# Weight conversion with its addition on VectorE, the verdict's reader moved, and natural copies by VectorE transposes

## The chip, the cores and the metric

The kernel runs on one core of a Trainium2 chip. The engines are named as in the profile: PE (TensorE, matmul and transpose; PEld is its weight load), DVE (VectorE), ACT (ScalarE), POOL (GpSimd) and SP (SyncE, whose queue issues the loads and stores). The metric is the device time of one execution in microseconds, median of several runs.

## What is computed

Three stages follow one another. All inputs are float32 but the two weight matrices of the middle stage, which are float64.

```python
# attention with a decaying state, B=4, H=8, S=768, D=48
for t in range(S):
    cur = einsum('bhd,bhe->bhde', u * k[t], v[t])
    y[t] = einsum('bhd,bhde->bhe', r[t], state + cur)
    state = w[t][..., None] * state + einsum('bhd,bhe->bhde', k[t], v[t])
x = y as 3072 tokens x 384

# feed-forward, 384 -> 2048 -> 384
h = x @ w_in
x = (h * (1.0 / (1.0 + exp(-1.702 * h)))) @ w_out

# mixture: 8 experts x 4 slots; phi is 384 x 32
logits = x @ phi
d = softmax of logits over the tokens
slots = d.T @ x                     # 32 x 384
out_slots[e] = relu(slots[e] @ w1[e]) @ w2[e]
c = softmax of logits over the slots
return c @ out_slots
```

## The kernel before

The tokens form 6 blocks of 512 (4 units of attention each, 24 units). A unit's attention is worked out on all engines and ends with `xth`/`xtl`, its tokens transposed and split into a high and a low part. A block's feed-forward walks over 16 slices f of the hidden width: h (L746, nine matmuls of xth and xtl with the slice's weights), the activation on ACT (L750, L754), its low part `glgh` on DVE (L758), and x (L766 to L768, nine matmuls), added up over f. What a block yields goes on to the mixture.

**Conversion** (`conv_nodes`, L468 to L506). A float64 weight arrives as two 32-bit words. For each of the 16 slices SP loads 768 KB of words into one of two `raw` buffers (L477); ACT takes the high word's magnitude into `cq` (L482) and scales the low word in place (L483); DVE clamps (L486), shifts and masks (L490) and puts the sign back (L494); one engine adds the low word's bits (L498); ACT writes the high part of the weight (L501) and DVE the low part (L504). A `raw` buffer is free when the addition has read it.

**Mixture, per block** (`moe2_nodes`, L786 to L916). Three copies (L802 on DVE, L804 on ACT) bring the block's x out of PSUM into `x2t`, with the model width on the partitions. From x2t PE makes the logits lg (L833). The natural copy `x2g`, with tokens on the partitions, is made by 12 PE transposes (L815) and four evictions (L819 on DVE or L821 on ACT). DVE takes the running maximum mb, mrun (L840, L844), ACT copies lg to lt (L836), PE transposes lt (ln, L848), DVE takes the row maximum rm and lc (L853, L854) and after the exponentials on ACT the normalised cnat (L870 to L873); en (L877) and es (L880) lead to pp (L885), which multiplies es with x2g and goes into prun (L892). After block 4 `scrA` (L1061, L1062) splits cnat, for the transposes cp (L1067).

**Verdict.** Limits of the number range are gathered while the kernel runs; inside0 (L1017 to L1020, DVE) folds them into `cm`, inside1 (L1023, POOL) takes the maximum over partitions, and inside2 (L1027, DVE) reads it into `outside`, which later decides whether a slower, careful path runs.

**Order.** Instructions stand in a fixed row on each engine. A planner writes these rows before the kernel is built: each step has a cost, a due time (`pr`) and sometimes a choice of engines with a cost for each (`C2E` for the addition), and steps marked `port` on DVE are not planned beside POOL. CONV0 and CONVD set the due times of the conversions, ATTD those of the attention units. Each engine works through its row in order: a row that waits holds up the rows behind it.

## Time and profile before

| what | us |
|---|---|
| median of 3 runs | 634.65 (633.98 to 636.14) |
| the profiled execution, own time | 633.73 |
| its span in the profile | 631.9 |
| PE busy | 570.4 |
| DVE busy | 431.6 |
| ACT busy | 274.9 |
| POOL busy | 90.3 |

The mean granted clock of TensorE is 0.99. The profiled execution is 1.8 us longer than its span; a change of the span is a change of the time. Busy shares are means over stages: attention of the first units until 66.84, block 0 among conversions until about 158, blocks 1 to 4 beside the attention of later units, block 5 and the last stage of the mixture. A row of the timeline or of a group gives, in brackets or at its end, how long its engine was idle just before it, and whose end released it. The end of a matmul is modelled, and matmuls overlap, so PE's pace is the distance of their starts.

### The profile page before, as it was taken

What the parts mean: (1) busy time and instruction counts of PE and PEld (TensorE: products, weight loads), DVE (VectorE), ACT (ScalarE), POOL (GpSimd) and SP (SyncE); (2) the same over time, 40 slices, a digit from 0 to 9 for tenths busy, and PEclk for the clock granted to TensorE, in tenths of its full rate; (3) what the DMA queues carried; (4) which work ended last, traced back from release to release, by engine and by line L of the source; (5) the groups of instructions that cost most, each with busy time, mean ns of one, the idle gap of its engine ahead of it and who ended that gap; (6) DMA issues with size and microseconds to landing.
All of it is one profiled execution on the core that took longest, in us unless ns stands there. A gap on an engine that the chain in (4) does not pass through costs nothing.

```text
span 631.9 us, 12380 instructions
## 1 busy us (share of the span) xinstructions
PE 570.4 (90%) x5092; PEld 462.7 (73%) x5092; DVE 431.6 (68%) x830; ACT 274.9 (44%) x524; POOL 90.3 (14%) x83
## 2 busy tenths in 40 slices
PE   3446899979999999999999999999999969999992
PEld 2445688767889999778877787877788757887362
DVE  9999797899999998787669766787672323112301
ACT  5544566573834443543316432444242333324232
POOL 3121232221111111111012202111120000000000
PEclk9999999999999999999999999999999989999997
DMA  8776434632343333032223232330210294467747
GB/s 294 233 240 209 140 104 158 215 150 76 115 114 114 107 108 113 7 107 74 91 76 101 55 110 77 101 113 28 74 39 1 95 357 147 153 229 249 306 152 219
DMA packets 29475, 86.08 MB, mean 136 GB/s; under 512 B 3040, under 2 KB 12384, under 8 KB 29408
## 3 DMA queue, kind: packets, MB, share of 16 engines
q1 hardware_dynamic: 29408, 85.19, 41.0%
q8 instruction: 42, 0.69, 0.5%
q14 instruction: 25, 0.20, 0.1%
HBM read 80.46 MB, written 4.72 MB: 135 GB/s over the span
## 4 chain that ended last, share of the span: by engine, by line
PE 74%; DVE 14%; issue 4%; DMA 3%; ACT 2%; POOL 1%; SPq 0%; ACTq 0%; DVEq 0%
PE h L746 28%; PE x L766 10%; PE x L767 9%; PE x L768 9%; PE y L652 5%; DMA raw<-in_wf_dram 2%; PE y L654 2%; PE aps L600 2%; PE so L1142 2%; PE eh L1100 2%; PE xps L668 1%; DVE glgh L758 1%; DVE at L574 1%; DVE at L552 1%; PE fo L1182 1%
## 5 line engine op out<-in xcount | busy, mean ns | idle before, releaser
L746 PE MATMUL h<-xth,w 128*128 128x512 f32 (+1 forms) x672 | 205.9, 371 | 3.2 <-ACT w L501 2.0
L750 ACT ACTIVATE ghgh<-h 128x512 fp32r<-128x512 f32 (+1 forms) x112 | 60.0, 537 | 231.7 <-PE h L746 171.0
L746 PEld LDWEIGHTS h<-xth,w 128*128 128x128 f32 x672 | 123.2, 191 | 25.8 <-ACT w L501 2.1
L766 PE MATMUL x<-ghgh,w 128*128 128x512 f32 (+1 forms) x336 | 125.7, 374 | 0.0
L746 PE MATMUL h<-xtl,w 128*128 128x512 f32 (+1 forms) x336 | 122.3, 364 | 0.5 <-DVE xtl L682 0.5
L767 PE MATMUL x<-glgh,w 128*128 128x512 f32 (+1 forms) x336 | 121.7, 362 | 0.6 <-DVE glgh L758 0.4
L768 PE MATMUL x<-ghgh,w 128*128 128x512 f32 (+1 forms) x336 | 121.4, 361 | 0.0
L758 DVE TENSOR_TENSOR glgh<-g,ghgh 128x512 fp32r<-128x512 f32 (+1 forms) x112 | 73.5, 657 | 55.4 <-ACT g L754 54.2
L766 PEld LDWEIGHTS x<-ghgh,w 128*128 128x128 f32 x336 | 63.9, 190 | 11.2 <-issue 0.6
L652 PEld LDWEIGHTS y<-vs,st 128*64 128x64 f32 (+2 forms) x768 | 55.0, 151 | 22.8 <-issue 13.2
L767 PEld LDWEIGHTS x<-glgh,w 128*128 128x128 f32 x336 | 63.9, 190 | 10.5 <-DVE glgh L758 1.9
L746 PEld LDWEIGHTS h<-xtl,w 128*128 128x128 f32 x336 | 64.2, 191 | 9.9 <-DVE xtl L682 1.4
L768 PEld LDWEIGHTS x<-ghgh,w 128*128 128x128 f32 x336 | 63.7, 190 | 9.6
L652 PE MATMUL y<-vs,st 128*64 128x48 f32 (+2 forms) x768 | 61.7, 238 | 9.0 <-DVE ind L551 4.7
L754 ACT ACTIVATE g<-h 128x512 f32<-128x512 f32 (+1 forms) x112 | 59.8, 534 | 4.8 <-DVE glgh L758 3.9
L654 PE MATMUL y<-vs,st 128*48 128x48 f32 (+2 forms) x704 | 50.1, 229 | 0.2 <-ACT st L622 0.2
L659 DVE TENSOR_TENSOR vs<-y,fl 48x384 f32<-48x384 f32 x44 | 24.4, 555 | 37.1 <-PE y L654 36.4
L498 POOL TENSOR_TENSOR cq<-cq,raw 128x768 int32<-128x768 int32 x16 | 32.1, 2008 | 112.2 <-DVE cq L494 52.2
L582 POOL TENSOR_TENSOR nat<-nat 128x384 f32<-128x384 f32 x16 | 16.2, 1012 | 217.4 <-DMA nat<-in_nat_dram 133.7
L654 PEld LDWEIGHTS y<-vs,st 128*48 128x48 f32 (+2 forms) x704 | 44.1, 133 | 0.8 <-ACT st L622 0.6
L600 PE MATMUL aps<-at 48*64 48x64 f32 x768 | 23.6, 239 | 20.5 <-DVE at L574 13.0
L612 DVE TENSOR_TENSOR st<-aps,mask 64x256 f32<-64x256 f32 (+1 forms) x80 | 37.8, 472 | 4.7 <-PE aps L600 3.7
(143 smaller groups left out, 695.8 us busy)
## 6 DMA issues: line engine op xcount, KB each, us to landing
w<-in_w_dram SPq DMA_DIRECT2D x32, 768.0 KB, 5.9
nat<-in_nat_dram SPq DMA_DIRECT2D x24, 576.0 KB, 3.8
raw<-in_wf_dram SPq DMA_DIRECT2D x16, 768.0 KB, 5.3
at<-in_ark_dram SPq DMA_DIRECT2D x24, 512.0 KB, 5.0
at<-in_aw_dram SPq DMA_DIRECT2D x24, 448.0 KB, 4.0
vs<-in_vr_dram SPq DMA_DIRECT2D x48, 96.0 KB, 2.9
out_dram<-ot SPq DMA_DIRECT2D x12, 384.0 KB, 4.0
ubt<-in_ub_dram SPq DMA_DIRECT2D x1, 192.0 KB, 7.5
```

Of the source, the lines that this page charges most:

```text
L498: onto[e].tensor_tensor(a, a, words(0), op=ALU.add)
L600: pe.matmul(ab[p if four else 0][vl:vh, col:col + CH], t_[a_][lo:hi, 1, 4 * g + h], t_[a_][lo:hi, 0, 4 * g + h], start=True, stop=True)
L612: ve.tensor_tensor(S[0][vl:vh, p, n * g:n * g + n, 0:CH], t_[kap[p if four else 0]][al:ah, 0:n * CH].rearrange("p (h t) -> p h t", h=n), m ...
L652: pe.matmul(yps[vl:vh, cols], S[0][0:k1, p, h, 0:CH], rhs, start=True, stop=True)
L654: pe.matmul(sps[ol:oh, cols], S[0][0:k1, p, h, CH:ROWS], rhs, start=True, stop=True)
L746: pe.matmul(h[:, :wd], a, b, start=(k == 0), stop=(k == len(seq) - 1))
L750: ac.activation(t_[kgh][0], t_[kh][:, :wd], AF.Gelu_apprx_sigmoid)
L754: ac.activation(t_[kg], t_[kh][:, :wd], AF.Gelu_apprx_sigmoid)
L758: ve.tensor_tensor(gl, t_[kg], gh.bitcast(F32), op=ALU.subtract)
L766: pe.matmul(o, whi, gh, start=(f == 0), stop=False)
L767: pe.matmul(o, whi, gl, start=False, stop=False)
L768: pe.matmul(o, wlo, gh, start=False, stop=(f == NF - 1))
```

## The change

- **Conversion.** The clamp (L486) is gone. The magnitude on ACT is scaled by 2^-112 and also summed over each partition into `wchk` (16 columns of the buffer `mx`), which inside0 tests with three more small operations. The shift has no mask; the sign's mask is one bit.
- **Addition.** `C2E` names DVE alone; in before's row all 16 stood on POOL. On DVE it is one instruction over 1536 halves of the 768 words.
- **Natural copies.** For the blocks in XND (1 to 4) the PE transposes and evictions are replaced by 16 DVE instructions (`xt32`), each of which transposes 4 x 3 blocks of 32x32 from x2t straight to x2g. Blocks 0 and 5 stay as they were.
- **Verdict.** inside1 is planned at 11.5 us and due early; its reader inside2 also waits for nsi, a step of the last stage, and is due last.
- **Planner.** CONV0, CONVD 0, 6 become 6, 4; ATTD 6 becomes 3.

```diff
@@ -30,12 +30,15 @@
 EPS = 1e-9
 W_TINY, W_HUGE = 2.0 ** -15, 122879.9921875
 F_MOST = 2.0 ** 40
+W_MOST = 2.0 ** -96
 RAWB, CQB, NEW = 2, 3, 8

 WIDE = (T, T // 2, T, T, T, T)

 KTU = (2, 3, 4, 5)
-C2E = {"DVE": 1.16, "POOL": 1.95}
+
+XND = (1, 2, 3, 4)
+C2E = {"DVE": 0.96}
 RUKE = ({"DVE": 1.12}, {"POOL": 2.1})
 QVE = ({"DVE": 0.56}, {"POOL": 1.05})
 PIECES = (192, 192)
@@ -44,8 +47,8 @@
 SOON = "w0 r0 c0 n0 u w1 r1 v0 n1 v1 w2 r2 n2 v2 c1 w3 r3 n3 v3"

 FIRST, SECOND, PERIOD, LAG, AHEAD = 42.0, 150.0, 82.0, 4.2, 74.0
-CONV0, CONVD, CONVL = 0.0, 6.0, 16.0
-ATT0, ATTD = 3.0, 6.0
+CONV0, CONVD, CONVL = 6.0, 4.0, 16.0
+ATT0, ATTD = 3.0, 3.0
 LAT = {"PE": 0.3, "ACT": 0.25, "DVE": 0.2, "POOL": 0.2, "DMA": 2.2, "X": 0.0}
 SAME = {"PE": 0.0, "ACT": 0.2, "DVE": 0.12, "POOL": 0.1, "DMA": 2.2, "X": 0.0}
 FROM = {"PE": 1.9, "ACT": 2.0, "DVE": 1.0, "POOL": 1.0, "DMA": 0.9}
@@ -388,6 +391,7 @@
     tick = cst.tile([P, 1], F32, name="tick")
     mfin = cst.tile([P, 1], F32, name="mfin")
     sm = {n: cst.tile([P, NSL], F32, name=n) for n in ("big", "mx", "rz")}
+    wchk = sm["mx"][:, 0:NF]
     chk = sm["rz"][0:ROWS, 0:NU * NB]
     ubt = ap1.tile([P, DM], F32, name="ubt")
     ind = ap1.tile([ROWS, NH, CH], F32, name="ind")
@@ -479,19 +483,17 @@
         def c0():
             wt[f] = wp.tile([P, 2, 2 * DM], F32R, tag="w", name=f"w{f}")
             t_[cq] = cp1.tile([P, 2 * DM], F32, tag="cq", name=cq, bufs=CQB)
-            ac.activation(t_[cq], words(1).bitcast(F32), AF.Abs)
+
+            ac.activation(t_[cq], words(1).bitcast(F32), AF.Abs, scale=2.0 ** -112, accum_out=wchk[:, f:f + 1])
             ac.activation(words(0), words(0).bitcast(U32), AF.Copy, scale=2.0 ** -29)
-
-        def c1a():
-            ve.tensor_scalar(t_[cq], t_[cq], W_TINY, W_HUGE, op0=ALU.max, op1=ALU.min)

         def c1b():
             a = t_[cq].bitcast(I32)
-            ve.tensor_scalar(a, a, 3, 0x3FFFFFF8, op0=ALU.logical_shift_left, op1=ALU.bitwise_and)
+            ve.tensor_scalar(a, a, 3, None, op0=ALU.logical_shift_left)

         def c1c():
             a = t_[cq].bitcast(I32)
-            ve.scalar_tensor_tensor(a, words(1), -0x40000000, a, op0=ALU.bitwise_and, op1=ALU.bitwise_or)
+            ve.scalar_tensor_tensor(a, words(1), -0x80000000, a, op0=ALU.bitwise_and, op1=ALU.bitwise_or)

         def c2(e):
             a = t_[cq].bitcast(I32)
@@ -504,8 +506,7 @@
             ve.tensor_tensor(wt[f][:, 1], t_[cq], wt[f][:, 0].bitcast(F32), op=ALU.subtract)

         n = N("DMA", 2.2, load, pr=soon(f"c{f}", pr - CONVL), take=[("raw", raw)])
-        n = N("ACT", 2 * act(2 * DM), c0, [n], pr, take=[("cq", cq), ("w", wk)], use=[raw])
-        n = N("DVE", dve(2 * DM, 1920), c1a, [n], pr, use=[cq], port=True)
+        n = N("ACT", 2 * act(2 * DM) + 0.2, c0, [n], pr, take=[("cq", cq), ("w", wk)], use=[raw])
         n = N("DVE", dve(2 * DM, 1920), c1b, [n], pr, use=[cq], port=True)
         n = N("DVE", dve(2 * DM), c1c, [n], pr, use=[raw, cq], port=True)
         n = N(C2E, 0, c2, [n], pr, use=[raw, cq], port=True)
@@ -820,8 +821,18 @@
                 else:
                     ac.activation(x2g()[:, j, 0:DM], t_[kt][:, :DM], AF.Copy)

+            if u in XND:
+                continue
             xns.append(N("PE", 0.33, xn, ts, pr(3.5), take=psum(kt)))
             ev.append(N({"DVE": dve(DM), "ACT": act(DM)}, 0, xg, [xns[-1], grp_last.get("pp")], pr(7.2), use=[kt]))
+
+        def xt32(q, s):
+            src = x2t()[32 * q:32 * q + 32, :, :, 32 * s:32 * s + 32]
+            dst = x2g()[32 * s:32 * s + 32, :, 0:DM].rearrange("p j (c d) -> p j c d", c=KC)[:, :, :, 32 * q:32 * q + 32]
+            ve.transpose(dst, src)
+
+        if u in XND:
+            ev = xns = [N("DVE", 0.57, lambda q=q, s=s: xt32(q, s), ts + [grp_last.get("pp")], pr(50)) for q in range(4) for s in range(4)]
         grp_last["xn"] = xns
         mo, mn = mrun[(u + 1) % 2], mrun[u % 2]
         klg, kln, ken, kpp = (f"{k}{u}" for k in ("lg", "ln", "en", "pp"))
@@ -1014,10 +1025,13 @@


     def inside0():
-        t_["cm"] = m2["ep"].tile([P, 2], F32, name="cm")
+        t_["cm"] = m2["ep"].tile([P, 3], F32, name="cm")
         ve.memset(t_["cm"], -1.0)
         ve.tensor_scalar(chk, chk, F_MOST, -1.0, op0=ALU.is_le, op1=ALU.mult)
         ve.tensor_reduce(t_["cm"][0:ROWS, 0:1], chk, axis=AX.X, op=ALU.max)
+        ve.tensor_scalar(wchk, wchk, W_MOST, -1.0, op0=ALU.is_lt, op1=ALU.mult)
+        ve.tensor_reduce(t_["cm"][:, 2:3], wchk, axis=AX.X, op=ALU.max)
+        ve.tensor_tensor(t_["cm"][:, 0:1], t_["cm"][:, 0:1], t_["cm"][:, 2:3], op=ALU.max)

     def inside1():
         gp.partition_all_reduce(t_["cm"][:, 1:2], t_["cm"][:, 0:1], P, reduce_op=bass_isa.ReduceOp.max)
@@ -1029,9 +1043,8 @@
     def inside3():
         t_["rv"] = nc.values_load(t_["out"][0:1, 0:1], min_val=0, max_val=1, skip_runtime_bounds_check_because="one less a comparison's 0 or 1")

-    n = nin = N("DVE", 0.35, inside0, limits + [nep], tend - 70)
-    n = N("POOL", 0.57, inside1, [n], tend - 29)
-    nok = N("DVE", 0.1, inside2, [n], tend - 28)
+    n = nin = N("DVE", 0.75, inside0, limits + [nep], tend - 70)
+    nout = N("POOL", 11.5, inside1, [n], tend - 70)

     G = grp_last
     n = N("DVE", 0.07, f0, [G["mx"]], tend - 59)
@@ -1046,6 +1059,7 @@
     nsi = N("POOL", 0.68, si0, [nep], tend - 40, take=[("xl", "scrB")])
     nsi = nsi0 = N("DVE", 0.17, f7, [n6, nz, nsi], tend - 59, use=["sp", "scrB"])

+    nok = N("DVE", 0.1, inside2, [nout, nsi], tend + 40)
     finish[0](nsi)


```

The names in the rows below carry the number of their buffer; at, ind, aps, st, vs and nat are buffers of the attention. The lines of the changed kernel lie a few off: the shift is L492, the sign's or L496, the addition L500, the last subtraction L506, glgh L759, the DVE transposes L832. DVE in block 0, about two conversions, before:

```order
L490 TENSOR_SCALAR cq_782<-cq_782 128x768
L574 TENSOR_TENSOR at_520<-at_520 112x1024
L494 SCALAR_TENSOR_TENSOR cq_782<-raw_746,cq_782 128x768
L486 TENSOR_SCALAR cq_835<-cq_835 128x768
L612 TENSOR_TENSOR st_96<-aps_0_853,mask 64x8x64 x2
L758 TENSOR_TENSOR glgh_7_0_850<-g_7_0_872,ghgh_7_0_849 128x512
L490 TENSOR_SCALAR cq_835<-cq_835 128x768
L582 TENSOR_TENSOR nat_584<-nat_584 128x384
L583 TENSOR_TENSOR nat_584<-nat_584,ubt 128x384
L504 TENSOR_TENSOR w_781<-cq_782,w_781 128x768
L494 SCALAR_TENSOR_TENSOR cq_835<-raw_801,cq_835 128x768
```

The same place now:

```order
L492 TENSOR_SCALAR cq_738<-cq_738 128x768
L506 TENSOR_TENSOR w_699<-cq_700,w_699 128x768
L496 SCALAR_TENSOR_TENSOR cq_738<-raw_703,cq_738 128x768
L759 TENSOR_TENSOR glgh_4_0_723<-g_4_0_772,ghgh_4_0_722 128x512
L500 ISA cq_738<-raw_703,cq_738 128x1536
L613 TENSOR_TENSOR st_96<-aps_0_741,mask 64x8x64 x2
L492 TENSOR_SCALAR cq_800<-cq_800 128x768
L506 TENSOR_TENSOR w_737<-cq_738,w_737 128x768
L496 SCALAR_TENSOR_TENSOR cq_800<-raw_759,cq_800 128x768
L759 TENSOR_TENSOR glgh_5_0_780<-g_5_0_821,ghgh_5_0_779 128x512
L500 ISA cq_800<-raw_759,cq_800 128x1536
L759 TENSOR_TENSOR glgh_6_0_825<-g_6_0_861,ghgh_6_0_824 128x512
```

The clamps are gone, and behind each or (L496) the addition (L500) stands in DVE's own row, one glgh later.

DVE at the turn from block 4 to block 5, from the verdict's first row on, before:

```order
L1062 TENSOR_TENSOR scrA<-cnat,scrA 128x8x32
L1018 MEMSET cm 128x2
L1019 TENSOR_SCALAR rz<-rz 112x24
L1020 TENSOR_REDUCE cm<-rz 112x1
L1027 TENSOR_SCALAR outside<-cm 128x1
L840 TENSOR_REDUCE mb_5328<-lg_5304 128x1
L844 TENSOR_SCALAR mrun_83<-mb_5328,mrun_84 128x1
L819 COPY x2g<-x2t_0_5322 128x384
L758 TENSOR_TENSOR glgh_0_0_5320<-g_0_0_5326,ghgh_0_0_5319 128x512
L819 COPY x2g<-x2t_2_5351 128x384
```

The same place now, from the row maximum on (ahead stand the six rows of the verdict, four of the block's 16 transposes, mb and mrun, and four more transposes):

```order
L864 TENSOR_REDUCE rm_5343<-ln_5320 128x4
L865 TENSOR_TENSOR lc<-ln_5320,rm_5343 128x128
L832 STREAM_TRANSPOSE x2g<-x2t 32x4x3x32 x7
L881 TENSOR_REDUCE zr_5365<-lc 128x4
L882 TENSOR_SCALAR zr_5365<-zr_5365 128x4
L883 RECIPROCAL zr_5365<-zr_5365 128x4
L884 TENSOR_TENSOR cnat<-lc,zr_5365 128x128
L891 COPY es<-en_5361 128x128
L832 STREAM_TRANSPOSE x2g<-x2t 32x4x3x32
L1075 CAST scrA<-cnat 128x8x32
L1076 TENSOR_TENSOR scrA<-cnat,scrA 128x8x32
L759 TENSOR_TENSOR glgh_0_0_5296<-g_0_0_5309,ghgh_0_0_5295 128x512
```

The reader `outside` is gone from the head of the row, and glgh_0, which stood third behind mrun, now comes behind all 16 transposes and the chain to es.

PE at the same turn, behind the last matmul of h_1, before:

```order
L746 MATMUL h_1_0_5335<-xth_4751,w_248 128x512
L815 MATMUL x2t_2_5351<-ident,x2t 128x128 x3
L815 MATMUL x2t_3_5358<-ident,x2t 128x128 x3
L848 MATMUL ln_5365<-ident,lt 128x128
L766 MATMUL x_5_0_5367<-ghgh_0_0_5319,w_139 128x512
L767 MATMUL x_5_0_5367<-glgh_0_0_5320,w_139 128x512
L768 MATMUL x_5_0_5367<-ghgh_0_0_5319,w_139 128x512
```

and now:

```order
L747 MATMUL h_1_0_5299<-xth_4730,w_229 128x512
L859 MATMUL ln_5320<-ident,lt 128x128
L1081 MATMUL cp_5322<-ident,scrA 128x128 x4
L747 MATMUL h_2_0_5331<-xth_4730,w_270 128x512
...
L747 MATMUL h_2_0_5331<-xth_4730,w_270 128x512
L888 MATMUL en_5361<-ident,et 128x128
L896 MATMUL pp_5374<-x2g,es 32x385 x4
L1081 MATMUL cp_5382<-ident,scrA 128x128 x4
L767 MATMUL x_5_0_5390<-ghgh_0_0_5295,w_139 128x512
L768 MATMUL x_5_0_5390<-glgh_0_0_5296,w_139 128x512
```

The transposes are gone, h_2 and the matmuls en, pp and cp stand ahead of x(0) (L767), which stood right behind ln. In the turns from block 1, 2 and 3 glgh_0 and glgh_1 stand among the first eight transposes, and glgh_2 behind all 16.

## Rows read from the trace of the kernel before

Times are in us from the start of the span, means in ns.

**Rows 1.** The page: busy us of each engine, share of the span, instructions

```profile
PE 570.4 (90%) x5092; PEld 462.7 (73%) x5092; DVE 431.6 (68%) x830; ACT 274.9 (44%) x524; POOL 90.3 (14%) x83
```

**Rows 2.** Windows: us; busy PE, PEld, DVE, ACT, POOL; clock; DMA share; GB/s

```profile
0.00:66.84 66.84, 31.11 (x413) 26.32 (x413) 61.73 (x106) 31.27 (x56) 13.77 (x16) 1.00 0.75 243
66.84:158.50 91.66, 86.19 (x630) 69.61 (x632) 79.18 (x114) 56.13 (x95) 22.48 (x12) 1.00 0.42 137
158.50:250.50 92.00, 91.45 (x1130) 86.20 (x1127) 85.06 (x180) 43.86 (x105) 16.07 (x16) 1.00 0.36 110
500.00:520.00 20.00, 15.14 (x89) 11.73 (x88) 6.61 (x21) 9.34 (x17) 1.78 (x5) 0.91 0.87 333
```

**Rows 3.** Timeline, PE, L746: start, duration, operands, idle before, releaser

```profile
66.84 0.79 PE L746 MATMUL h<-xth,w 128*128 128x512 f32 x1 [0.58 <-ACT xth L679]
...
128.77 0.50 PE L746 MATMUL h<-xth,w 128*128 128x512 f32 x1 [1.96 <-ACT w L501]
```

**Rows 4.** Groups by form: count | busy us, mean ns | idle, releasers

```profile
L498 POOL TENSOR_TENSOR cq<-cq,raw 128x768 int32<-128x768 int32 x16 | 32.1, 2008 | 112.2 <-DVE cq L494 52.2 <-ACT st L622 21.9 <-DMA vs<-in_vr_dram 10.1
...
L494 DVE SCALAR_TENSOR_TENSOR cq<-raw,cq 128x768 int32<-128x768 int32 x16 | 15.2, 950 | 0.0
...
L486 DVE TENSOR_SCALAR cq<-cq 128x768 f32<-128x768 f32 x16 | 13.4, 835 | 4.4 <-ACT cq L482 4.2
...
L490 DVE TENSOR_SCALAR cq<-cq 128x768 int32<-128x768 int32 x16 | 8.8, 553 | 0.0
...
L570 ACT ACTIVATION_READ_ACCUMULATOR at<-at 112x1 f32 x24 | 4.8, 198 | 0.0
```

**Rows 5.** Timeline, 14.7 to 29 us: DVE rows beside additions on POOL

```profile
15.04 1.93 DVE L590 TENSOR_TENSOR nat<-nat,q 128x384 f32<-128x384 f32 x1
...
26.73 1.85 POOL L498 TENSOR_TENSOR cq<-cq,raw 128x768 int32<-128x768 int32 x1 [10.18 <-DVE cq L494]
...
27.19 1.81 DVE L486 TENSOR_SCALAR cq<-cq 128x768 f32<-128x768 f32 x1 [0.59 <-ACT cq L482]
```

**Rows 6.** Timeline, 107 to 110 us: an addition and the next raw load

```profile
107.47 2.11 POOL L498 TENSOR_TENSOR cq<-cq,raw 128x768 int32<-128x768 int32 x1 [5.69 <-DVE cq L494]
...
109.60 0.37 SPq L477 DMA_DIRECT2D raw<-in_wf_dram  x1
```

**Rows 7.** Waits, SyncE queue: us in total, times, longest

```profile
SPq L477 <- POOL cq L498: 47.8, 10, 9.8
```

**Rows 8.** Groups by line and form, three shapes on DVE

```profile
L574 DVE TENSOR_TENSOR at<-at 112x1024 f32<-112x1024 f32 x24 | 29.9, 1245 | 0.4
...
L637 DVE STREAM_TRANSPOSE st<-at 32x256 f32<-32x256 f32 x64 | 27.9, 435 | 1.4
...
L641 DVE STREAM_TRANSPOSE st<-at 32x32 f32<-32x32 f32 x32 | 5.1, 161 | 0.0
```

**Rows 9.** Timeline, PE, the turn from block 2 to block 3

```profile
340.96 0.82 PE L815 MATMUL x2t<-ident,x2t 128*128 128x128 f32 x6
...
341.61 0.27 PE L848 MATMUL ln<-ident,lt 128*128 128x128 f32 x1
```

**Rows 10.** Timeline, the turn from block 4 to block 5

```profile
500.87 1.97 ACT L804 ACTIVATE x2t<-x 128x512 f32<-128x512 f32 x3 [0.21 <-PE x L768]
...
512.57 0.15 DVE L1027 TENSOR_SCALAR outside<-cm 128x1 int32<-128x1 f32 x1 [9.94 <-POOL cm L1023]
...
513.28 0.42 PE L848 MATMUL ln<-ident,lt 128*128 128x128 f32 x1 [4.71 <-ACT lt L836]
...
513.37 0.77 PE L766 MATMUL x<-ghgh,w 128*128 128x512 f32 x1
...
520.11 0.39 PE L746 MATMUL h<-xtl,w 128*128 128x512 f32 x1
...
520.34 0.62 PE L746 MATMUL h<-xth,w 128*128 128x512 f32 x2
...
524.21 0.85 PE L885 MATMUL pp<-x2g,es 128*32 128x385 f32 x8
```

## The prediction, made before the changed kernel ran

> **What bounds the kernel now.** I read the page first, then windows, then groups by line and form, then waits and the timeline at two places. TensorE (PE) is busy 570.4 us of a span of 631.9 [rows 1], so only a stretch where PE waits, or work taken off PE, can shorten the run. The windows say where PE waits [rows 2]: up to 66.84 us it is busy 31.1 us while VectorE (DVE) is busy 61.73, so DVE carries that stretch; from 66.84, the first feed-forward matmul [rows 3], to 158.5, the end of block 0, PE is busy 86.19 of 91.66, so 5.5 us are idle; from 158.5 to 250.5 it is full (91.45 of 92.00) and DVE has 7 us to spare; in 500 to 520, the turn from block 4 to block 5, PE does 15.14 of 20. The change works in exactly these places, and the sum has four terms.
>
> **The conversion's prices.** Sixteen conversions run, each now clamp, shift, or, add, last subtraction [rows 4]. The clamp L486 goes: its free price is that of the shift L490, same shape, 0.553 us; its mean of 0.835 holds a stretch that the next paragraph explains. The shift without its mask and the other sign mask leave L490 and L494 as they are. ScalarE's L482 gets a read of its accumulator; the same read costs 0.198 at L570 [rows 4], so 16 x 0.2 = 3.2 us on an engine that works 31.27 of the first 66.84 us [rows 2], hidden but for 0.2 in each conversion's chain. The addition leaves GpSimd (POOL), 2.008 us x16, and becomes one row on DVE over 1536 halves of 768 words. No row of before shows it. Lower bound: 0.95, L494, the same 768 words with the same interleaved operand. Upper bound: one half per element at the rate of L574, 1.245 us for 1024 [rows 8], is 1.87. I take 0.95, because L494 is nearest in operands and words, and keep 1.87 for a rival. The Trainium skill, page "VectorE: DVE Perf Modes", section "What auto-detection actually checks", lets a two-source operation on 16-bit values run at twice the rate only where every tensor steps by one; the low words here are every second word, so by that rule the add runs at the single rate, and by the page's 0.96 GHz it would take an estimated 1.6 us and some overhead. That is rival two; no run here shows it yet.
>
> **Term 1, up to the first h matmul.** By the order, up to the last xtl of block 0 DVE issues 6 clamps, 6 shifts, 6 ors and 5 subtractions before, and 0, 5, 5 and 4 with 4 adds after; attention rows are equal in number. At 0.553 for clamp and shift and 0.95 for or and subtraction (which has the or's shape) that is 3.32 + 0.55 + 0.95 + 0.95 = 5.77 less, and 4 x 0.95 = 3.80 more: 1.97 less, or 1.7 when each of the 101 rows there before and of the 96 after is priced by its own group; I take 1.7. Besides, a POOL add slows the DVE row that it meets: L486 takes 1.81 at 27.19 beside the add of 26.73 [rows 5], 1.26 over its free price. Three such rows lie before 66.84; the first is L590 at 15.04, 1.93 where the others of its shape take 0.55, and they hold some 3.5 us (1.38, 1.26 and 0.9). With no add on POOL they fall away. 1.7 + 3.5 = 5.2, and since DVE carries this stretch it shows in full: the first h at about 61.6. Bounds: 1.5 with adds at 1.87 (4 x 0.92 dearer), 6 at most.
>
> **Term 2, block 0.** Two raw buffers feed the conversions; the next load is issued as the add ends (107.47 + 2.11, load at 109.60 [rows 6]), and SyncE's queue waits 47.8 us on the add in ten places [rows 7]. PE meets this as a late weight: 1.96 us idle before L746 at 128.77 [rows 3]. From load to load a conversion loses the clamp (0.84 with stretch) and 1.06 of the add, and gains 0.2: 1.7 shorter, with two buffers 0.85 per conversion, 8.5 for ten. PE can take back no more than its 5.5 us idle, and part of that is attention. The order also moves PE's attention work for units 6 and 7 from among block 0's matmuls to behind them: block 0 shortens and block 1, where PE is full, grows by as much, which enters the sum at nothing. I take 3.3, between 0 (the load, not the add, is late) and 6.
>
> **Term 3, three turns (blocks 1 to 3).** Before, PE transposes in 12 rows per block; six of them at 340.96 are followed by the next matmul at 341.61 [rows 9], 0.65, so 1.3 per block leaves a full PE. Four evictions go too, and 16 DVE transposes of 384 elements come. L637 has 256 in 0.435 and L641 32 in 0.161 [rows 8]: 1.22 ns an element, hence 0.59; 9.4 us per block, against 7 us of DVE's 92 that were idle from 158.5 to 250.5 and two or so that the evictions free: it fits, though narrowly. Bounds: 0.44 (256 elements alone), and above, 12 single blocks at 0.161, 1.93, which L637's 8 blocks in 0.435 speak against. They must be done before pp, the matmul that reads x2g. By the order, DVE has between the copies into x2t and es, which pp reads too, some 12 us: 9.4 of transposes, two glgh, and the small rows mb to cnat. PE has in front of pp lg, three h and two x (nine matmuls each, 0.23 us apart, 520.11 to 520.34 [rows 10], so five times 2.07) and some attention: about 12 us as well. It is just covered. 3 x 1.3 = 3.9; without cover each 0.1 us more per transpose puts 1.6 us before each pp.
>
> The same page, sections "The three transpose paths" and "Rules for kernel authors", tells authors to put a 128x128 transpose on TensorE when PSUM is a fitting destination, and gives VectorE 32x32 blocks only; this speaks against the change. Its 0.39 us on TensorE would make the 12 an estimated 4.7 us; the trace shows 12 in 1.3, and the row decides. What the rule threatens is rival three.
>
> **Term 4, the turn from block 4 to 5.** Before, the verdict's reader L1027 stood at 512.57 waiting 9.94 us for POOL, the maximum mb behind it, and PE waited 4.71 for lt until 513.28 [rows 10]. Moved back, it releases mb. But what is late next is the transposes. x2t is ready at 502.84 (500.87 + 1.97 [rows 10]). In DVE's new row stand, from 503.2 on (after six verdict rows): 4 transposes, mb and mrun, 4, rm and lc, 7, zr to cnat, es, 1, and only after two scrA rows glgh_0. At 15 x 0.59 + 0.5 + 0.6 + 0.9 + 0.3, es is done at 514.4; the last transpose frees pp at about 515.0, two scrA and glgh_0 x(0) at about 516.3. PE, with lg, h_1, ln, cp, h_2 and en in front, runs dry at about 510 (before at 513.28 - 4.71 = 508.57; less 1.3, plus h_2, cp and en): an idle of 5 us or more where 4.71 stood. But h_2, en, pp and two cp are done by then, which before came later: before, x(0), x(1), h_2, h_3 and pp were through at 525.06 (524.21 + 0.85); after, x(0), x(1) and h_3 end at 516.3 + 3 x 2.07 = 522.5, plus some 1.2 for the slow matmuls that follow such an idle (0.77 at 513.37 [rows 10]), 523.7. The gain is 1.4, that of the PE transposes (bounds -2 to 6). Moving the reader thus pays almost nothing itself. At its new place, after the last block's lc, its 0.15 us [rows 10] has POOL's result long before, and only a zr waits behind it.
>
> **Sum.** 5.2 + 3.3 + 3.9 + 1.4 = 13.8. From the profiled 633.73 that is 619.9; the median of the runs is 634.65, 0.92 higher, so 620.8.
>
> **Rivals.** One: term 4 keeps the whole wait. If the transposes run at 0.30, the 15 rows shrink by 4.4 us and the idle all but vanishes: 13.8 + 4.4 = 18.2, so 616.4. For: L641 shows 32 elements in 0.161, mostly fixed cost; against: L637's slope and the order. Two: the add costs 1.87. Term 1 falls to 1.5, and in block 0 eleven adds bring 10 us to a DVE busy 79.18 of 91.66 [rows 2], so term 2 is nought: 1.5 + 3.9 + 1.4 = 6.8, hence 627.9; for it, 1536 halves in the row; against, L494. Three, the slower side: DVE transposes with a destination scattered in 32-word pieces are dearer than 0.59 and stand before four pp. Sixty-four times the excess must eat 13.8, so from 0.59 + 0.22 = 0.81 on the kernel is slower; at 0.87 it is 17.9 - 13.8 = 4.1 slower, 638.8. For: no row has this shape; against: L637, eight blocks in one row, costs 0.054 a block. Four: the change doesn't act, because the run takes its fallback or PE's start hangs on loads (16 x 768 KB and attention's in 66 us at 243 GB/s, [rows 2]) rather than DVE, and the transposes' gain is lost at pp: 634 to 635.
>
> **How the numbers follow.** Forecast 0.55 (617 to 624.5, from terms 1 and 2 between their bounds), rival one 0.10 (612 to 617), two 0.22 (624.5 to 633), three 0.08, four 0.05. A measurement of this kernel tells some 0.3%, 1.9 us, from no change. Faster: 0.55 + 0.10 + 0.21 = 0.86; same: 0.05 + 0.01 = 0.06; slower 0.08. Leaving out three, four and the upper third of two (0.07), the range is 612 to 630.
>
> **What would show it.** Right: first h near 61.6 and no DVE row of 1.5 us or more beside an add; L500 near 0.95; L832 near 0.59; PE without idle at pp in the turns 1 to 3; at 4 to 5 an idle of about 5 us before pp or x instead of before ln. Wrong: L500 above 1.4 (rival two), L832 above 0.75 with idle before pp in four places (three), a first h later than 65, or an idle of under 1 us at 4 to 5 (one).

## The result, and the profile after

The changed kernel takes 616.37 us (median of 4 runs, 614.20 to 620.15); the kernel before, beside it, 635.39. The ratio is 0.9703 with a 95% interval of 0.9645 to 0.976, so 2.4 to 3.6% faster. Forecast were 620.8 us, 612 to 630. The profiled execution took 614.20 with a span of 612.4; it is the fastest of the four, so the profile shows the new kernel at its best.

The page's lines on the engines, the slices of PE, DVE and POOL, and the chain that ended last (of after, against [rows 1]):

```profile
PE 561.3 (92%) x5044; PEld 455.4 (74%) x5044; DVE 458.9 (75%) x889; ACT 274.5 (45%) x532; POOL 60.1 (10%) x67
...
PE   2565999999999999999999999999999969998992
...
DVE  9999997999998899998979998698963661212301
...
POOL 2000000000130121022120311111210000000000
...
PE h L747 29%; PE x L767 10%; PE x L768 10%; PE x L769 10%; PE y L653 5%; DVE x2g L832 3%; DMA raw<-in_wf_dram 3%; PE aps L601 2%; PE y L655 2%; PE so L1156 2%; PE eh L1114 2%; PE xps L669 1%; PE fo L1196 1%; DVE cq L500 1%; DVE glgh L759 1%
```

DVE works 27 us more and the kernel is 19.5 us shorter: what counted was where DVE stood in the way, not how much it did. POOL does 4.1 us of work up to 142.30, where 36 stood up to 158.50 before [rows 2], and the DVE transposes (L832) have come into the chain.

The stages up to block 2, as windows (of after, against [rows 2]; PE, PEld, DVE, ACT, POOL):

```profile
0.00:60.34 60.34, 29.46 (x412) 25.13 (x413) 56.30 (x99) 29.31 (x57) 4.01 (x11) 0.92 0.79 250
60.34:142.30 81.96, 80.81 (x566) 64.70 (x567) 74.31 (x113) 58.72 (x106) 0.11 (x1) 0.97 0.51 160
142.30:236.50 94.20, 94.20 (x1188) 89.73 (x1187) 85.66 (x184) 44.49 (x107) 14.98 (x17) 1.00 0.35 109
```

The groups on which the terms were built (of after, against [rows 4] and [rows 8]):

```profile
L832 DVE STREAM_TRANSPOSE x2g<-x2t 32x384 f32<-32x384 f32 x64 | 36.5, 570 | 1.0
...
L496 DVE SCALAR_TENSOR_TENSOR cq<-raw,cq 128x768 int32<-128x768 int32 x16 | 15.2, 952 | 0.1
L500 DVE CUSTOM_DVE_ANT_0 cq<-raw,cq 128x1536 uint16<-128x1536 uint16 x16 | 15.2, 950 | 0.0
...
L492 DVE TENSOR_SCALAR cq<-cq 128x768 int32<-128x768 int32 x16 | 8.8, 551 | 2.8 <-ACT cq L487 2.7
...
L487 ACT ACTIVATION_READ_ACCUMULATOR cq<-raw 128x1 f32 x16 | 3.1, 196 | 0.0
```

The three new prices are 0.950 us for the addition (taken as 0.95), 0.570 for a transpose (0.59) and 0.196 for the read of the accumulator (0.198).

**Where the time went.** To compare kernels I cut each profile at four marks that all of them have: the start of ACT's first activation (ghgh) of block 0, of block 2 and of block 5, and that of its last in block 5; the end of the span closes the last stage. Between the first two marks PE has the same work in both kernels, whatever the order moves inside. Times are from the timelines; stages in us.

| kernel | ratio to before | to block 0 | to block 2 | to block 5 | block 5 | rest |
|---|---|---|---|---|---|---|
| before | | 71.25 | 179.05 | 253.98 | 71.90 | 55.7 |
| changed | 0.9703 | 65.03 | 171.49 | 249.51 | 70.92 | 55.5 |
| difference | | -6.2 | -7.6 | -4.5 | -1.0 | -0.2 |
| forecast (terms 1 to 4) | | -5.2 | -3.3 | -3.9 | -1.4 | 0 |
| r1_plan_cost | 0.9638 | 65.96 | 170.82 | 249.56 | 64.21 | 57.5 |
| r2_xnd123_plan | 0.9634 | 66.46 | 171.00 | 249.54 | 65.11 | 56.3 |
| r3_reader_only | 0.9891 | 71.30 | 178.18 | 253.83 | 65.11 | 57.3 |
| r4_no_dve_transposes | 0.9708 | 65.75 | 171.45 | 253.28 | 65.88 | 57.7 |
| r5_add_on_pool | 0.9819 | 66.25 | 176.09 | 251.74 | 70.93 | 56.5 |
| r6_clamp_back | 0.9852 | 66.72 | 179.63 | 250.30 | 71.02 | 56.2 |
| r7_old_dates | 0.9811 | 74.98 | 170.33 | 251.18 | 71.15 | 56.9 |
| r8_new_dates_only | 1.0129 | 69.46 | 187.06 | 253.92 | 72.29 | 59.5 |
| r9_no_xnd_plan | 0.9722 | 66.54 | 174.85 | 253.34 | 65.12 | 59.4 |
| r10_double_transposes | 1.0143 | 65.96 | 171.12 | 284.62 | 65.12 | 57.4 |
| r11_clamp_gone | 0.9870 | 71.52 | 173.28 | 250.72 | 71.38 | 58.4 |
| r12_changed_again | 0.9712 | 65.45 | 173.85 | 249.53 | 70.22 | 56.3 |

The last three stages are sharp: kernels with the same order there agree within some 0.2 us to block 5 and 0.7 in block 5. The stage to block 2 is less so: among the seven kernels with the changed conversion and dates (changed, r1, r2, r4, r9, r10, r12) it goes from 170.82 to 171.49 in five and is 173.85 in r12 and 174.85 in r9. Those two have 3.4 us at a granted clock of 0.50 there (117.0 to 120.5 and 119.2 to 122.6), right behind an idle of PE of 1.43 and 1.75 us for glgh, and the other five have none. r3, r6 and r8 have such a stretch in that stage too, so 2 to 4 us of a difference to them can be this. All later marks of a kernel move with it. "Dates" are the planner's numbers CONV0, CONVD and ATTD.

### The profile page after: what moved, and what is told of

Same layout as the page of the kernel before. It is cut to its first block, busy times and chain, and to the rows that moved or that the text cites. A ratio compares the mean times of both kernels' runs of the same rounds, so it can differ in the third digit from the quotient of the medians.

```text
span 612.4 us, 12355 instructions
## 1 busy us (share of the span) xinstructions
PE 561.3 (92%) x5044; PEld 455.4 (74%) x5044; DVE 458.9 (75%) x889; ACT 274.5 (45%) x532; POOL 60.1 (10%) x67
## 4 chain that ended last, share of the span: by engine, by line
PE 77%; DVE 14%; DMA 3%; issue 2%; ACT 2%; SPq 0%; ACTq 0%; DVEq 0%
PE h L747 29%; PE x L767 10%; PE x L768 10%; PE x L769 10%; PE y L653 5%; DVE x2g L832 3%; DMA raw<-in_wf_dram 3%; PE aps L601 2%; PE y L655 2%; PE so L1156 2%; PE eh L1114 2%; PE xps L669 1%; PE fo L1196 1%; DVE cq L500 1%; DVE glgh L759 1%
## 5 line engine op out<-in xcount | busy, mean ns | idle before, releaser
L767 PE MATMUL x<-ghgh,w 128*128 128x512 f32 (+1 forms) x336 | 125.5, 374 | 0.0
L759 DVE TENSOR_TENSOR glgh<-g,ghgh 128x512 fp32r<-128x512 f32 (+1 forms) x112 | 72.4, 646 | 60.9 <-ACT g L755 59.4
L767 PEld LDWEIGHTS x<-ghgh,w 128*128 128x128 f32 x336 | 63.8, 190 | 11.0 <-issue 1.0
L653 PEld LDWEIGHTS y<-vs,st 128*64 128x64 f32 (+2 forms) x768 | 53.6, 149 | 16.6 <-issue 8.7
L755 ACT ACTIVATE g<-h 128x512 f32<-128x512 f32 (+1 forms) x112 | 59.6, 533 | 14.1 <-DVE glgh L759 13.8
L653 PE MATMUL y<-vs,st 128*64 128x48 f32 (+2 forms) x768 | 59.9, 236 | 2.2 <-DVE st L613 1.1
L601 PEld LDWEIGHTS aps<-at 48*64 48x64 f32 x768 | 20.1, 148 | 25.0 <-DVE at L575 16.9
L832 DVE STREAM_TRANSPOSE x2g<-x2t 32x384 f32<-32x384 f32 x64 | 36.5, 570 | 1.0
```

Source lines behind the costliest of these rows:

```text
L601: pe.matmul(ab[p if four else 0][vl:vh, col:col + CH], t_[a_][lo:hi, 1, 4 * g + h], t_[a_][lo:hi, 0, 4 * g + h], start=True, stop=True)
L653: pe.matmul(yps[vl:vh, cols], S[0][0:k1, p, h, 0:CH], rhs, start=True, stop=True)
L755: ac.activation(t_[kg], t_[kh][:, :wd], AF.Gelu_apprx_sigmoid)
L759: ve.tensor_tensor(gl, t_[kg], gh.bitcast(F32), op=ALU.subtract)
L767: pe.matmul(o, whi, gh, start=(f == 0), stop=False)
L832: ve.transpose(dst, src)
```

## The turn from block 4 to block 5: the reader, the transposes and one planned cost

In the new profile the wait is where the forecast put it (timeline; start, duration, idle before):

```profile
487.69 2.32 DVE L832 STREAM_TRANSPOSE x2g<-x2t 32x384 f32<-32x384 f32 x4
488.90 0.27 PE L859 MATMUL ln<-ident,lt 128*128 128x128 f32 x1
...
490.68 4.07 DVE L832 STREAM_TRANSPOSE x2g<-x2t 32x384 f32<-32x384 f32 x7
...
492.06 0.33 PE L888 MATMUL en<-ident,et 128*128 128x128 f32 x1 [0.36 <-ACT et L868]
...
495.73 0.28 DVE L891 COPY es<-en 128x128 f32<-128x128 f32 x1
496.03 0.58 DVE L832 STREAM_TRANSPOSE x2g<-x2t 32x384 f32<-32x384 f32 x1
...
496.75 1.51 PE L896 MATMUL pp<-x2g,es 128*32 128x385 f32 x8 [4.36 <-DVE x2g L832]
...
498.96 0.78 PE L767 MATMUL x<-ghgh,w 128*128 128x512 f32 x1
499.54 0.63 PE L768 MATMUL x<-glgh,w 128*128 128x512 f32 x1
```

ln no longer waits for POOL's maximum; PE runs dry behind en and waits 4.36 us for the last transpose, where 4.71 stood [rows 10]. The matmuls behind it are slow again (0.58 apart at first, where 0.23 is the pace). That is the granted clock, which stood at 0.50, the lower of its two levels (1.2 GHz). The windows (PE, PEld, DVE, ACT, POOL, clock), one of the kernel before and two of after:

```profile
513.40:516.80 3.40, 3.25 (x8) 2.26 (x9) 3.01 (x8) 3.37 (x8) 0.00 (x0) 0.50 1.01 418
```

```profile
496.75:501.40 4.65, 4.65 (x18) 2.92 (x19) 3.05 (x7) 1.19 (x2) 0.00 (x0) 0.50 0.45 183
501.40:504.00 2.60, 2.60 (x13) 2.15 (x12) 0.43 (x1) 1.09 (x2) 0.00 (x0) 1.00 0.25 31
```

In the kernel before PE had done nothing for 4.7 us and had just begun again when the clock fell, at 513.4; in the changed kernel it fell at 494.6, while PE waited. Half of what PE works at 0.50 is lost, an estimate from these windows: 1.6 us before and 2.3 after. Four runs take this place apart.

**The reader alone.** The kernel before, its reader moved:

```diff
-    nok = N("DVE", 0.1, inside2, [n], tend - 28)
+    nout = n
...
+    nok = N("DVE", 0.1, inside2, [nout, nsi], tend + 40)
     finish[0](nsi)
```

> The kernel before with nothing changed but the verdict's reader, which moves from the head of DVE's row to behind nsi. Theory: DVE no longer stands behind POOL's maximum, PE's 4.71 us idle before ln goes with the slow matmuls behind it: 5 to 6 us faster than before, near 629. Rival: lt, the exponentials or the evictions are late next and the wait only changes its name: under 2 us.

Measured: 627.02 us, 0.9891 (0.9873 to 0.9909), 6.7 us faster, and all of it in block 5: 71.90 to 65.11. The rows that had waited, now (timeline of r3_reader_only):

```profile
504.13 0.29 DVE L840 TENSOR_REDUCE mb<-lg 128x1 f32<-128x128 f32 x1 [2.48 <-PE lg L833]
...
507.43 0.27 PE L848 MATMUL ln<-ident,lt 128*128 128x128 f32 x1
...
510.98 0.38 POOL L1023 PARTITION_ALL_REDUCE cm<-cm  x1 [10.24 <-DVE scrA L1063]
...
516.46 0.85 PE L885 MATMUL pp<-x2g,es 128*32 128x385 f32 x8
```

mb waits for lg, as it should, and POOL's maximum comes late as ever but nobody waits for it. PE has no idle over 0.3 us in the block. The granted clock stays at 1.00 through the block. So the reader's wait was worth 6.8 us: the 4.71 listed, some 1.6 of matmuls at half the clock, and half a microsecond of other changes, a little more than expected.

**The planned cost of POOL's maximum.** The changed kernel books inside1 at 11.5 us; this keeps `port` steps of DVE away from it in the plan, and glgh_0 lands behind all transposes. One number is put back:

```diff
-    nout = N("POOL", 11.5, inside1, [n], tend - 70)
+    nout = N("POOL", 0.57, inside1, [n], tend - 70)
```

> The changed kernel with one number different: the planner books POOL's maximum (inside1) at 0.57 us as before and not at 11.5. All rows up to the turn from block 4 to block 5 stay; there glgh_0 and glgh_1 move ahead among the transposes, and on PE x(0), h_2, h_3 and x(1) come ahead of pp. Theory (the transposes took the place of the reader's wait, and only what PE has in front of pp decides): the 4.36 us idle before pp goes, about 4 us faster than the changed kernel, some 612 us where it has 616. Rival (DVE is simply full there, so what is put first only delays the rest): the idle moves to pp or to another x and the time stays within 1 us of the changed kernel.

Measured: 610.70 us, 0.9638 (0.9615 to 0.9661), and the changed kernel again beside other runs 0.9712 (0.9675 to 0.9748): 0.7%, near 5 us. The rows of r1_plan_cost at the same place:

```profile
488.59 0.69 DVE L759 TENSOR_TENSOR glgh<-g,ghgh 128x512 fp32r<-128x512 f32 x1
489.21 0.27 PE L859 MATMUL ln<-ident,lt 128*128 128x128 f32 x1
...
489.67 0.48 PE L767 MATMUL x<-ghgh,w 128*128 128x512 f32 x1
...
490.56 4.07 DVE L832 STREAM_TRANSPOSE x2g<-x2t 32x384 f32<-32x384 f32 x7
...
496.53 1.75 DVE L832 STREAM_TRANSPOSE x2g<-x2t 32x384 f32<-32x384 f32 x3
...
498.59 0.85 PE L896 MATMUL pp<-x2g,es 128*32 128x385 f32 x8
```

The same transposes end 1.7 us later than in the changed kernel and pp runs 1.8 us later, without any idle: glgh_0 stands at 488.59, so PE does x(0), h_2, h_3 and x(1) in front of pp. PE stays busy, and the clock stays at its higher level (window of r1_plan_cost):

```profile
489.00:499.00 10.00, 9.93 (x52) 7.38 (x50) 9.57 (x22) 6.54 (x11) 0.38 (x1) 1.00 1.01 416
```

Block 5 falls from 70.92 to 64.21, by 6.7 us: the 4.36 of idle and the 2.3 lost to the clock.

**PE transposes at that turn, and everywhere.** r2 has DVE transposes in blocks 1 to 3 alone, r4 in none, with the planned cost as changed; r9 is r2 without any.

```diff
-XND = (1, 2, 3, 4)
+XND = (1, 2, 3)
...
-    nout = N("POOL", 11.5, inside1, [n], tend - 70)
+    nout = N("POOL", 0.57, inside1, [n], tend - 70)
```

> As the run before, and block 4's natural copies by PE transposes as in the old kernel (blocks 1 to 3 by DVE). Theory: no wait left at the turn from 4 to 5 but PE does 1.3 us more, so 1.3 us slower than the run before if that one has no idle there, and some 3 us faster than the changed kernel. Rival: DVE's 9 us still hold up glgh in the run before; then this one is the faster of the two by 1 to 3 us.

And r4; r9 has inside1 at 0.57 as well:

```diff
-XND = (1, 2, 3, 4)
+XND = ()
```

> The changed kernel with the natural copies of all blocks by PE transposes and evictions again; conversion, reader and planner numbers stay as changed. Theory: at the turns from block 1, 2 and 3 PE gets 1.3 us each back, 3.9; at the turn from 4 to 5 1.3 more on PE against the 4.36 us idle before pp, which goes or shrinks, as x(0) still stands behind es: between 1 and 5 us slower than the changed kernel, 617.5 to 621. Rival (the DVE transposes cost more than they save): faster than the changed kernel.

> The changed kernel without DVE transposes in any block and with POOL's maximum booked at 0.57 us, so that glgh_0 stands early at the turn from 4 to 5. Against r2_xnd123_plan (0.9634 of before) it lacks only the DVE transposes of blocks 1 to 3. Theory: PE gets 1.3 us a turn back, 3.9 in all, about 0.9695 of before. Rival (DVE's 9 us a block cost as much as they save): 0.963 to 0.965.

r2 measures 610.26 us, 0.9634 (0.9602 to 0.9666), no other than r1 by the clock, and 0.9 us longer in block 5, against 1.3 of PE work. r4 measures 615.51, 0.9708 (0.9679 to 0.9737), the same as the changed kernel, where 1 to 5 us slower was expected. The table says why: without DVE transposes the stage to block 5 is 3.8 us longer (253.28 against 249.51), and block 5 is 5.0 shorter (65.88 against 70.92): PE does the transposes and still has no idle over 0.39 us, and the clock stays at 1.00. The expectation had left out that the clock's loss goes with the idle. What the 48 transposes of blocks 1 to 3 brought, the 16 of block 4 took, by an order in which PE could not work past them. The Trainium skill's advice to transpose on TensorE (page "VectorE: DVE Perf Modes", section "Rules for kernel authors") thus held for block 4 as it was planned and not for blocks 1 to 3. r9 against r2 in the stage to block 5 is 253.34 against 249.54, 3.8 us for three turns; its median, 618.40 (0.9722, 0.9673 to 0.9772), where about 0.9695 was expected, lies further off. Its profile, of the slowest of its four runs, is also 3.9 longer up to block 2, where the two kernels have the same rows, and 3 longer in the rest; in both places it has stretches at half the clock that r2's has not. The verdict of r9 thus rests on the stage, not on the median.

## Is the cover of the transposes thin?

r10 is r2 with each DVE transpose of blocks 1 to 3 issued twice.

```diff
             ve.transpose(dst, src)
+            ve.transpose(dst, src)
```

> As r2_xnd123_plan, but each DVE transpose of blocks 1 to 3 is issued twice, 9.1 us more on DVE at each of three turns, the order unchanged. Theory (just covered, narrowly): the copies are late then, PE idles 6 to 9 us before pp at each of the three turns, and the time is some 15 to 27 us longer than r2. Rival (DVE has slack there): under 6 us longer.

Measured: 643.68 us, 1.0143 (1.0089 to 1.0197), 33 us longer than r2, more than expected. All of it is in the stage to block 5, 284.62 against 249.54: 35.1 us for 48 x 0.57 = 27.4 us of DVE work. PE's three rows of pp (timeline of r10_double_transposes):

```profile
262.28 1.51 PE L897 MATMUL pp<-x2g,es 128*32 128x385 f32 x8 [7.63 <-DVE x2g L833]
...
354.30 1.51 PE L897 MATMUL pp<-x2g,es 128*32 128x385 f32 x8 [5.44 <-DVE x2g L833]
...
451.54 1.51 PE L897 MATMUL pp<-x2g,es 128*32 128x385 f32 x8 [7.38 <-DVE x2g L833]
```

PE is idle 27.1 us in the stage to block 5, against 0.9 in r2, about as much as was added. The rest is the granted clock, which fell to 0.50 in each of the three idles (windows of r10, columns as above):

```profile
257.20:267.40 10.20, 5.12 (x44) 3.51 (x45) 9.50 (x18) 0.60 (x1) 1.20 (x1) 0.50 0.03 9
352.80:359.60 6.80, 5.30 (x17) 3.04 (x17) 6.48 (x14) 0.61 (x2) 0.00 (x0) 0.50 0.01 2
448.30:458.60 10.30, 7.06 (x33) 5.00 (x34) 9.66 (x20) 0.60 (x1) 1.45 (x1) 0.50 0.01 2
```

PE worked 17.5 us in them, so some 8.7 were lost: 26.2 and 8.7 are the 35 us. There was no slack to speak of. Rival three had the right mechanism; it stayed away because the transposes took 0.570 us and not 0.81.

## The start and block 0: clamp, addition and dates

Each part was undone alone in the changed kernel, the dates were put alone into the kernel before, and the clamp alone was left out (with additions on POOL and old dates). The planner makes a new order in each, so the parts don't add up.

The additions (r5):

```diff
-C2E = {"DVE": 0.96}
+C2E = {"POOL": 1.95}
```

> The changed kernel with the sixteen additions on POOL again; conversion without clamp, planner numbers, reader and DVE transposes stay. Theory (the addition's gain is the stretch it put on DVE rows and the raw buffer it held for 2.0 us): the first h matmul stays within 1 us, as DVE loses 3.8 us of adds and gets 3.5 of stretch back, and block 0 loses more: the first h of block 2 comes 3 to 6 us later than in the changed kernel (236.5), the time is 3 to 6 us longer. Rival (the gain lies in the clamp and the new order): within 1.5 us.

The clamp (r6), with limits that change no value:

```diff
+        def c1a():
+            ve.tensor_scalar(t_[cq], t_[cq], 0.0, W_HUGE, op0=ALU.max, op1=ALU.min)
...
+        n = N("DVE", dve(2 * DM, 1920), c1a, [n], pr, use=[cq], port=True)
         n = N("DVE", dve(2 * DM, 1920), c1b, [n], pr, use=[cq], port=True)
```

> The changed kernel with a clamp row of the old shape in each conversion again (0.55 us x16 on DVE, limits that change no value). Theory by the terms of the forecast: five clamps before the first h put it 2.8 us later, and block 0 loses up to 3 us more; 3 to 5 us longer in all. Rival (DVE's row holds enough waits there to hide them): under 1.5 us.

The dates (r7; r8 has the opposite edit, in the kernel before):

```diff
-CONV0, CONVD, CONVL = 6.0, 4.0, 16.0
-ATT0, ATTD = 3.0, 3.0
+CONV0, CONVD, CONVL = 0.0, 6.0, 16.0
+ATT0, ATTD = 3.0, 6.0
```

> The changed kernel with the old planner numbers for conversions and attention units (CONV0, CONVD 0, 6; ATTD 6). Theory (only the work counts): within 2 us of the changed kernel, the first h included. Rival (the order makes it: units overlap, and attention leaves block 0): block 0 again loses some 8 us against PE's work, and the time is over 4 us longer.

> The kernel before with the new planner numbers alone (CONV0, CONVD 6, 4; ATTD 3). Theory: within 2 us of before, since DVE carries the start and its work is the same. Rival (the order makes it): over 4 us faster.

r11 joins the edits of r5 and r7; r12 is the changed kernel as it is.

> The changed kernel with the additions on POOL and the old planner numbers, so that in the first 240 us only the clamp's going is left of the change. Theory, corrected after the runs so far (DVE sets the pace until block 2, so what leaves DVE shows in full): the clamps took 13.4 us of DVE, and block 2's first h, at 250 us before, comes 8 to 13 us earlier. Rival (the chain load, ACT, DVE, POOL per raw buffer sets it): under 5 us earlier.

> The changed kernel once more, beside the runs of this call, to put r1_plan_cost and r2_xnd123_plan against it: 0.970 of before. At the turn from 4 to 5 again 4 to 5 us idle before pp.

Block 2 begins (sum of the first two stages) at 250.30 before and at 236.52 in the changed kernel.

- **r6, clamp back:** 246.35, 9.8 us later, for 16 x 0.55 = 8.8 us of DVE work; 625.79 us, 0.9852 (0.9778 to 0.9927). Expected were 3 to 5. Only 1.7 of it lie ahead of the first activation of block 0. The profile has a stretch at half the clock from 109.4 to 112.9, behind an idle of 1.79; against r12 (239.30), which has one too, r6 is 7 later.
- **r5, additions on POOL:** 242.34, 5.8 later, 1.2 of it at the start; 623.36 us, 0.9819 (0.9749 to 0.9889). As expected up to block 2; the time is 7 us longer, a little more than expected.
- **r7, old dates:** 245.31, 8.8 later, and nearly all at the start (74.98 against 65.03); 622.73 us, 0.9811 (0.9727 to 0.9895). The theory, that only the work counts, fell. The rival had the size but not the place: its stage to block 2 is even 1.2 shorter than that of the changed kernel.
- **r8, new dates alone:** 256.52, 6.2 later than before; 643.97 us, 1.0129 (1.0062 to 1.0196). Neither theory expected a loss. Up to the first activation r8 gains 1.8, and then its stage to block 2 is 8.0 longer, with 2.49 us of idle on PE for a late weight at 129.16; the new dates didn't suit the longer conversion.
- **r11, of the conversion's changes the clamp's going alone:** 244.80, 5.5 earlier than before, where 8 to 13 was expected and under 5 by the rival; 626.33 us for the whole kernel, 0.987 (0.9836 to 0.9904), most of the rest from the stage to block 5.
- **r12:** 616.83 us, 0.9712 (0.9675 to 0.9748), with 4.37 us idle before pp.

The windows of r6 show how full DVE is (PE, PEld, DVE, ACT, POOL, as above):

```profile
0.00:62.00 62.00, 30.41 (x412) 26.06 (x412) 57.85 (x103) 29.06 (x57) 4.02 (x11) 1.00 0.74 238
62.00:142.80 80.80, 77.51 (x490) 62.41 (x491) 73.27 (x112) 53.20 (x96) 0.11 (x1) 0.98 0.48 158
142.80:246.30 103.50, 101.46 (x1264) 94.57 (x1263) 96.32 (x201) 49.83 (x117) 18.12 (x17) 1.00 0.36 109
```

DVE is busy 227.4 us of 246.3 here, 216.3 of 236.5 in the changed kernel and 226.0 of 250.5 before [rows 2]: some nine tenths in all three. The clamp put back costs 11.2 us of DVE and 7 to 10 of time. So work on DVE can count until block 2 and not only until the first h matmul, as the prediction had it, through stretches in which PE counts as full. How much DVE works doesn't settle the time, though: up to block 2 DVE is busy 214.8 us in r5, less than in the changed kernel, and r5 is 5.8 later; r8 has the 226 of before and is 6.2 later than before; and r11, which was to come 8 to 13 earlier if what leaves DVE shows in full, came 5.5. Its place in the row counts as well. What changed most is the pace of the conversions; their last subtractions in the new kernel, fourth and sixteenth (timeline):

```profile
59.17 0.95 DVE L506 TENSOR_TENSOR w<-cq,w 128x768 fp32r<-128x768 f32 x1
...
129.76 0.95 DVE L506 TENSOR_TENSOR w<-cq,w 128x768 fp32r<-128x768 f32 x1
```

That is 5.88 us for each of twelve. Before, the fifth stood at 63.23 and the last at 151.00, 7.98 for each of eleven. The cycle still runs through the raw buffers: the queue waits for the addition as before, and a load starts as an addition ends (of after: the queue's row, against [rows 7], and a place in the timeline, against [rows 6]):

```profile
SPq L481 <- DVE cq L500: 45.1, 12, 6.9
```

```profile
74.16 0.95 DVE L500 CUSTOM_DVE_ANT_0 cq<-raw,cq 128x1536 uint16<-128x1536 uint16 x1
...
75.18 0.37 SPq L481 DMA_DIRECT2D raw<-in_wf_dram  x1
```

From a load to the second next, which takes the same buffer, it is 16.65 us before and 12.01 now (mean of nine, from the sixth load on), 4.6 less. Of that 3.5 lie between the end of the magnitude on ACT and the end of the or on DVE, 7.57 before and 4.03 now (means over the sixth to the last conversion). In r11 these are 5.18, 2.4 less than before for a clamp that took 0.84: with a row went waits in DVE's row.

## Why the prediction was right, and where it was not

**Prices: right.** The clamp (0.551 where r6 puts it back), the addition at 0.950, the read at 0.196 and the transposes at 0.570 all came within 4% of what was taken. Rival two is gone: the addition takes 1536 halves, one operand of which steps over every second word, in the time of 768 words. The rule in the Trainium skill, page "VectorE: DVE Perf Modes", section "What auto-detection actually checks", had made it an estimated 1.6 us at the single rate; the row says 0.950, and the measurement decides.

**Term 1, the start: right in size** (6.2 by the mark, 6.5 by the first h matmul at 60.34, for 5.2). Its two causes are less sure than they were told. Up to the first h matmul DVE is busy 56.30 us where 61.73 stood, 5.4 less, and no DVE row before 150 us is stretched beside POOL now, as forecast. But r7 has no additions on POOL either and starts at 74.98, later than before; r11 has them and none of the clamps and starts at 71.52, as before. The order that the new dates make decides how many conversions stand in front of the first h; the forecast read that order row by row, which is why its sum held.

**Term 2, up to block 2: the mis-sized term,** 7.6 for 3.3. The step that failed is "PE can take back no more than its 5.5 us idle". A matmul's end in the trace is modelled and a delayed one counts as busy, so PE's idle is a lower bound of what PE loses. An estimate: priced at the distance of their starts in undisturbed stretches (0.23 us for an h or x matmul), PE's rows from the first to the sixteenth activation of block 0 fill 64.8 of the 74.6 us before, 9.8 lost, and 66.7 of 70.1 in the changed kernel, 3.4 lost. With every row at the median distance that its form has in blocks 2 and 3, the losses are 10.9 and 5.2; the granted clock is 1.00 throughout in both. The price in front of it was too small as well. The mechanism, the raw buffer's cycle, is there in both kernels, but the cycle lost 4.6 us where 1.7 was forecast: the forecast priced the rows that go and not the waits in DVE's row that went with them. Before, PE met late weights [rows 3], and the last subtraction ended at 151.9, behind block 0's last activation (145.9); now it ends at 130.7, in front of it (135.1). Of the parts tried here, none gives the 13.8 us that the first two stages have gained: the clamp alone 5.5, the dates alone -6.2. What the addition is worth depends on the dates: with old ones nothing that can be seen (r11 to r7, 244.80 to 245.31), with new ones 5.8 (r5). How the planner's order brings this about was not taken apart, and so the cause of the 4.3 us that term 2 missed is shown in part only.

**Term 3, three turns: right.** 4.5 in the stage, 3.8 by r9 against r2, for 3.9. The transposes were just covered, and r10 shows how little was left.

**Term 4, the turn from 4 to 5: right in size and mechanism,** 1.0 for 1.4. The reader's wait, worth 6.8 us alone, came back as a wait for the transposes, with 4.36 us idle. The slow matmuls behind it, taken at 1.2, cost some 2.3, since the clock stayed at 0.50 for longer than before; rival one (616) named what would be won without it, and r1 won it and more by another way, 6.7 us in block 5, without a cheaper transpose: by glgh_0 in front of eleven of the sixteen.

**The sum** was 13.8 and the profile gave 19.5, of which term 2 has 4.3 that were not forecast, term 1 1.0, term 3 0.6, term 4 -0.4 and the rest 0.2: 5.7 more than forecast. Against the median of the kernel before beside it the changed kernel gains 19.0. So 616.37 lies inside the range but just outside the forecast's own band (617 to 624.5), in that of rival one (612 to 617). Rival one didn't happen, since a transpose took 0.570 us and not 0.30 and the idle stayed; the time is down there because of term 2. Rival four counts all 16 raw loads in the first 66 us, where the trace of before has seven; nothing else hangs on that.

**A better kernel.** r1 (0.9638) and r2 (0.9634) both beat the changed kernel; r1 differs from it by one planned cost.

## What to carry to other kernels

A listed idle of the busiest engine is a lower bound of its loss: where operands come late, its matmuls stretch and count as busy, and behind a wait the granted clock may be down. So set its work at its best pace against the time that passed, and read the clock behind each wait, before you cap a gain. When a wait is taken off a row, read the new row for what stands in it instead, and look for work that the waiting engine could do in front of it; here one planned cost decided whether block 5 won 7.7 us or 1.0. And planner dates belong to the costs that they were set with: the new dates alone made the old kernel slower.

## What was not expected of the hardware

The granted clock of TensorE fell to 0.50 behind the waits of the last sections, and besides it differed between kernels that have the same rows up to there. Windows of the changed kernel (first three) from 50 to 65 us, with PE lightly used in the first two:

```profile
50.00:55.00 5.00, 2.34 (x40) 1.91 (x36) 4.86 (x9) 2.16 (x5) 0.00 (x0) 0.59 1.02 314
55.00:60.00 5.00, 1.59 (x15) 1.06 (x13) 4.92 (x8) 1.24 (x3) 0.00 (x0) 0.50 0.82 268
60.00:65.00 5.00, 4.28 (x10) 3.14 (x11) 4.97 (x10) 2.84 (x5) 0.00 (x0) 0.55 0.92 269
```

and of r2_xnd123_plan:

```profile
55.00:60.00 5.00, 1.85 (x32) 1.70 (x33) 4.89 (x9) 1.85 (x3) 0.00 (x0) 1.00 0.76 264
60.00:65.00 5.00, 4.03 (x10) 2.65 (x11) 4.97 (x10) 2.31 (x5) 0.00 (x0) 1.00 0.90 278
```

The clock fell to 0.50 (1.2 GHz) in one and stayed at 2.4 GHz in the other, and it cost nothing that can be seen, since DVE sets the pace there: block 0's first activation is at 65.03 with the fall and at 66.46 without. In the last stage it does cost. The same happens behind pp and its two neighbours in the last block, r1_plan_cost first, the changed kernel second:

```profile
560.00:564.00 4.00, 3.59 (x24) 1.62 (x27) 3.00 (x12) 0.31 (x1) 0.00 (x0) 0.62 0.27 110
```

```profile
566.40:570.40 4.00, 3.59 (x36) 1.86 (x39) 3.00 (x12) 0.31 (x1) 0.00 (x0) 1.00 0.30 121
```

Both windows begin 1.8 us behind the start of pp, at the same matmuls; PE gets through 24 of them at 0.62 and 36 at 1.00. Over all fourteen profiles the length of the rest goes with such stretches between pp and the last matmuls: the seven without one take 55.5 to 56.9 us, the four with 3.4 us at 0.50 take 57.3 to 57.7, the three with 6.8 us take 58.4 to 59.5. So 1 to 3 us of a run's time hang on what it meets there. What sets it was not settled.
